# Recurrent attention beside a gated MLP: another order of loads and relays ahead of the first scores

## The chip, the cores and the metric

The kernel runs on one core of a Trainium2 chip. The time is device microseconds of that core; lower is better. Three runs of the kernel before took 367.76, 369.17 and 369.84 us, with a median of 369.17 us. One further execution was profiled. It took 366.92 us, and the span from its first to its last instruction is 364.8 us. The engines are named as in the profile: PE is TensorE's matmul and PEld its weight load, DVE is VectorE, ACT is ScalarE, POOL is GpSimd, SP is SyncE. SPq and ACTq are the queues of SP and ACT that issue DMAs.

## The reference

The input x has 2048 rows of 640 in bf16. Rows are normalized, and two branches read them. Branch A is attention with 32 heads of 20 in 4 segments of 512 rows: causal softmax within a segment, and a memory M, z that earlier segments left. Branch B is a gated MLP of width 1536.

```
xn = layernorm(x)
# branch A, for each segment s (512 rows):
logits = qs @ ks.T * scale + causal mask;  a_dot = softmax(logits) @ vs
a_mem  = (phi(qs) @ M) / (phi(qs) @ z + 1e-6)      # phi(t) = t + 1 if t > 0 else exp(t)
o      = g * a_mem + (1 - g) * a_dot               # g = sigmoid(beta), one number a head
M += phi(ks).T @ vs;  z += sum(phi(ks))
s = concat(o) @ wo
# branch B:
h = sigmoid(xn @ w_gate) * (xn @ w_up);  g = silu(h @ w_down)
out = x + s * g
```

## The kernel before, in words

The program is one straight list of instructions for each engine; an engine works through its list in order. The source emits the instructions, and their order in the source is their order on each engine. Two parts emit them: `startup()` (L514 to L557) by hand, for what comes ahead of the first scores, and the loop at L607, which walks 4 segments x 24 slots. A slot emits one `scores` unit, then fill work, then `weigh` of the unit before. Fill work has two sources: a heap of tasks with a due time in slots (`at`, `later`) and the list `bulk` of `gate`, `up` and `down` pieces. `take(k)` emits the first k pieces of `bulk` at once.

The names that matter here:

- `x_load(n, p)` (L105) loads rows of segment n: two chunks of 128 rows x 640 (160 KB each) as two DMAs for segment 0, as one DMA of 320 KB for later segments. Segment 0's four chunks are issued on SP's queue. Wv (800 KB) and beta are issued on ACT's queue, Wk and Wq (800 KB each), the first third of w_gate (`Wg[0]`) and of w_up (`Wu[0]`) (640 KB each) on SP's (L115 to L131). All these stand at the very start of both queues.
- `warm()` runs WARM = 36 matmuls of the identity on PE, ahead of the first real ones.
- `ln_stats` is five small DVE and POOL steps for each chunk: two halves of statistics (L199, L200), their sum (L201), and the reciprocal root on POOL (L202, L203). `ln_norm` writes the normalized chunk xn (L210). In segment 0, PE transposes it (L217) and ACT copies it to xnT (L218); in later segments a DMA transpose on SP's queue does (L220).
- `v_pair` emits the v projection (L305), `k_chunk` (L244) and `q_chunk` (L269) those of K and Q; ACT copies the results in segment 0 (L233, L309).
- The scores need Q and K with another assignment of rows to partitions, and this goes through DRAM: `stage_out` stores K or Q in two parts (L258), `relay` loads each half back in four DMAs of 80 KB (L229) into KT or QT. Row 20 of each head's strip of QT holds a bound for the softmax: `q_bound` computes it on PE (L281) and ACT copies it to cb (L284); `c_out` stores it (L292, 32 KB) and `c_in` loads it into both QT tiles (L299). All of these DMAs are on SP's queue. The first scores (L459) read KT, QT and that row.
- `load_glu(i, which)` (L128) loads third i of w_gate or w_up. Pieces `gate(n, f)` and `up(n, f)` use third f // 4. `load_late` loads Wd (1920 KB) and Wo (800 KB).
- `gate` ends in a tanh on ACT (L380), `up` in a product on DVE (L390). `phi` is three steps on DVE and ACT for each of five chunks of K (L315, L316, L319, L323); its transposed result goes to `pkt` by DMA (L327).

In `startup()` SP's queue has this order after the first weights: both stores of K, relay of K half 0, `load_glu(1, 0)`, relay of K half 1, both stores of Q, relay of Q half 0, `c_out`, relay of Q half 1, `c_in`, `load_glu(1, 1)`, the rows of segment 1. PE has, behind the last q chunk: `v_pair(3)`, `q_bound`, then three gates and three ups of `bulk` (`take(1)`, `take(5)`), then the first scores.

Each DMA counts its landing on one of eight semaphores. The framework deals them out in turn, over both queues, and a DMA that is given one waits until the DMA that had it before has landed.

Of the kernel before, what the change touches and what calls it, by code (L numbers as in the profile page):

```python
# [9 lines left out]
P = 128  # L10
# [3 lines left out]
DH = 20  # L14
# [29 lines left out]
    [(2, 0, 256, 256)],  # L44
]

WARM = 36
SHARE = (1.15, 1.15, 0.7)
NSLOT = NG * len(UNITS)

# [2 lines left out]
def kernel(  # L53
# [14 lines left out]
    nc = tc.nc  # L68
    x2 = A_x.flatten_outer_dims()
# [16 lines left out]
    Cs = [dpool.tile([H, L], BF, name=f"Cs{i}") for i in range(2)]  # L86
# [8 lines left out]
    def at(time, cost, fn, *a):  # L95
        count[0] += 1
        heapq.heappush(tasks, (time, count[0], cost, fn, a))

    def later(lag, fn, *a):
        at(clock[0] + lag, 0.0, fn, *a)  # L100
# [4 lines left out]
    def x_load(n, p):  # L105
        t = lnp.tile([P, 2, D], BF, name="xt2")
        st[n][f"x{p}"] = t
        r0 = n * L + 2 * p * P
        if n == 0:
            for i in range(2):  # L110
                nc.sync.dma_start(t[:, i, :], x2[r0 + i * P:r0 + (i + 1) * P, :])
        else:
            nc.sync.dma_start(t[:], x2[r0:r0 + 2 * P, :].rearrange("(i p) d -> p i d", p=P))

    x_load(0, 0)  # L115
    x_load(0, 1)
    W = {}
    beta_b = cpool.tile([P, H], BF, name="beta_b")
# [7 lines left out]
    def load_glu(i, which):  # L126
        w, src = ((Wg, B_w_gate), (Wu, B_w_up))[which]
        nc.sync.dma_start(w[i][:], src[:, i * L:(i + 1) * L].rearrange("(c p) n -> p c n", p=P))  # L128
# [20 lines left out]
    QT = [cpool.tile([P, 4, L], BF, name=f"QT{i}") for i in range(3)]  # L149
# [5 lines left out]
    def v_ones(a, b):  # L155
        for i in range(a, b):
            nc.gpsimd.memset(V[i][:, :, DH:VW], 1.0)

    def make_ind():

        nc.gpsimd.memset(nInd[:], -1.0)
        nc.gpsimd.affine_select(out=nInd[:], in_=nInd[:], compare_op=ALU.is_ge, fill=0.0,
                                base=0, pattern=[[P, DC], [-DH, H]], channel_multiplier=1)
        nc.gpsimd.affine_select(out=nInd[:], in_=nInd[:], compare_op=ALU.is_ge, fill=0.0,
                                base=DH - 1, pattern=[[-P, DC], [DH, H]], channel_multiplier=-1)
# [24 lines left out]
    def ln_stats(n, p, i0=0, i1=2):  # L190
        s = st[n]
        x = s[f"x{p}"]
        if i0 == 0:
            s[f"mv{p}"] = lnp.tile([P, 2, 2], F32, name="mv")
            s[f"rstd{p}"] = lnp.tile([P, 2], F32, name="rstd")
        mv, rstd = s[f"mv{p}"], s[f"rstd{p}"]
        for i in range(i0, i1):
            bs = lnp.tile([P, 2, 6], F32, name="bs")
            nc.vector.bn_stats(bs[:, 0, :], x[:, i, 0:HB])  # L199
            nc.vector.bn_stats(bs[:, 1, :], x[:, i, HB:D])  # L200
            nc.vector.bn_aggr(mv[:, i, :], bs[:])  # L201
        nc.gpsimd.tensor_scalar(rstd[:, i0:i1], mv[:, i0:i1, 1], EPS, None, op0=ALU.add)  # L202
        nc.gpsimd.tensor_tensor(rstd[:, i0:i1], rstd[:, i0:i1], nhalf[:, i0:i1], op=ALU.pow)  # L203

    def ln_norm(n, p, i):
        s = st[n]
        if "xnT" not in s:
            s["xnT"] = xpool.tile([P, DC, L], BF, name="xnT")
        xn = lnp.tile([P, D], BF, name="xn")
        nc.vector.tensor_scalar(xn[:], s[f"x{p}"][:, i, :], s[f"mv{p}"][:, i, 0:1], s[f"rstd{p}"][:, i:i + 1],  # L210
                                op0=ALU.subtract, op1=ALU.mult)
        j = 2 * p + i
        dst = s["xnT"][:, :, j * P:(j + 1) * P]
        if n == 0:
            pT = ps_d.tile([P, DC, P], BF, name="pT", tag="d")
            for c in range(DC):
                nc.tensor.transpose(pT[:, c, :], xn[:, c * P:(c + 1) * P], ident[:])  # L217
            nc.scalar.copy(dst, pT[:])  # L218
        else:
            later(0.7, lambda: nc.sync.dma_start_transpose(dst, xn[:]))  # L220


    def half_tile(tiles, n, half):
        return tiles[(2 * n + half) % 3]

    def relay(n, half, src, dst):
        rows = src[n % 2].rearrange("(g r d) n -> r d g n", r=4, d=DH)
        for r in range(4):
            nc.sync.dma_start(half_tile(dst, n, half)[32 * r:32 * r + DH, :, :], rows[r][:, 4 * half:4 * half + 4, :])  # L229
# [26 lines left out]
    def stage_out(n, half, src, dst, name):  # L256
        a, b = ((0, 3), (3, 5))[half]
        nc.sync.dma_start(src[n % 2][a * P:b * P, :].rearrange("(c p) n -> p c n", p=P), st[n][name][:, a:b, :])  # L258
        if n:
            later(1.0, relay, n, half, src, dst)  # L260
# [28 lines left out]
            c_out(n, cb)  # L289

    def c_out(n, cb):
        nc.sync.dma_start(Cs[n % 2][:, :], cb[:])  # L292
        if n:
            later(1.0, c_in, n)

    def c_in(n):
        rows = Cs[n % 2].rearrange("(g r) n -> r g n", r=4)
        for half in range(2):
            nc.sync.dma_start(half_tile(QT, n, half)[DH:P:32, :, :], rows[:, 4 * half:4 * half + 4, :])  # L299

    def v_tile(n, j, half):
        s = st[n]
# [197 lines left out]
    def take(k):  # L500
        for _, fn, a in bulk[:k]:
            fn(*a)
        del bulk[:k]

    def warm():
        ps = ps_d.tile([P, L], F32, name="wps", tag="d")
        for i in range(WARM):
            nc.tensor.matmul(ps[:, 0:P], lhsT=ident[:], rhs=ident[:], start=True, stop=True)

    def v_pair(j):  # L510
        for h in range(2):
            v_tile(0, j, h)

    def startup():  # L514
        warm()
        nc.gpsimd.memset(KT[0][:], 1.0)
        ln_stats(0, 0, 0, 1)
        ln_stats(0, 0, 1, 2)
        ln_norm(0, 0, 0)
        v_ones(0, 4)  # L520
        ln_stats(0, 1, 0, 1)
        ln_norm(0, 0, 1)
        v_pair(0)
        ln_stats(0, 1, 1, 2)
        ln_norm(0, 1, 0)
        v_pair(1)
        ln_norm(0, 1, 1)
        v_pair(2)
        make_ind()
        nc.gpsimd.memset(KT[1][:], 1.0)  # L530
        for c in range(DC):
            k_chunk(0, c)
        nc.gpsimd.memset(KT[2][:], 1.0)
        stage_out(0, 0, Ks, KT, "k5")
        for c in range(DC):
            q_chunk(0, c)
            if c == 0:
                stage_out(0, 1, Ks, KT, "k5")
                relay(0, 0, Ks, KT)
                load_glu(1, 0)  # L540
            elif c == 2:
                relay(0, 1, Ks, KT)
                stage_out(0, 0, Qs, QT, "q5")
        make_bd()
        v_ones(4, 8)
        v_pair(3)
        stage_out(0, 1, Qs, QT, "q5")
        relay(0, 0, Qs, QT)
        q_bound(0)
        relay(0, 1, Qs, QT)  # L550
        c_in(0)
        take(1)
        gates()
        take(5)
        load_glu(1, 1)
        x_load(1, 0)
        x_load(1, 1)  # L557

    startup()
    at(0.9, 0, load_glu, 2, 0)  # L560
# [5 lines left out]
    for n in range(NSEG):  # L566
        w = NSLOT * n
        m = n + 1
        if m < NSEG:
            for p in range(2):  # L570
                at(w + 0.2 + 3 * p, 0.1, ln_stats, m, p)
                for i in range(2):
                    at(w + 1.2 + 3 * p + 0.3 * i, 0.1, ln_norm, m, p, i)
            for i in range(8):
                at(w + (5.2 if i < 4 else 6.2) + 0.5 * i, 0.68, v_tile, m, i // 2, i % 2)
            for c in range(DC):
                at(w + 9.6 + 0.75 * c, 1.08, k_chunk, m, c)
                at(w + 13.4 + 0.75 * c, 1.08, q_chunk, m, c)
                at(w + 12.6 + 0.8 * c, 0.0, phi, m, "k5", c)
                at(w + 18.8 + 0.7 * c, 0.0, phi, m, "q5", c)  # L580
            at(w + 17.2, 1.12, q_bound, m)
            if m + 1 < NSEG:
                for p in range(2):
                    at(w + 16.1 + p, 0.0, x_load, m + 1, p)
            if n == 0:
                for c in range(DC):
                    at(0.3 + 0.8 * c, 0.0, phi, 0, "k5", c)
            for i, cs in enumerate(([0, 1, 2], [3, 4])):
                at(w + 8.9 + i, 0.6, m_update, n, cs)
        if n >= 1:  # L590
            for j in range(4):
                at(w + 1.1 + 0.3 * j, 0.0, o_ready, n - 1, j)
                if j < 2:
                    at(w + 4.0 + j, 0.0, xr_load, n - 1, j)
            for i in range(8):
                at(w + 6.6 + i, 0.68, o_proj, n - 1, i // 2, i % 2)
                at(w + 3.0 + 0.75 * i, 0.35, mem_read, n, i // 2, i % 2)
# [52 lines left out]
    n = NSEG - 1  # L650
# [43 lines left out]
```

## Time and profile before

| what | us |
|---|---|
| median of three runs | 369.17 |
| the profiled execution | 366.92 |
| its span | 364.8 |
| PE busy in the span | 340.2 |
| ACT busy | 234.6 |
| DVE busy | 228.2 |
| POOL busy | 103.7 |
| first statistics on DVE (row chunk 0 there) | 3.24 |
| first v matmul on PE | 10.29 |
| first K matmul on PE | 16.73 |
| first Q matmul on PE | 22.13 |
| first scores on PE | 40.06 |
| second, third scores on PE | 43.93, 49.33 |

A row of the timeline has its start, its duration, the engine, the line in the kernel, the operation with output and input, how many of them were merged, and in brackets the time that the engine sat idle before it with what ended that. Line numbers are those of the kernel before. A span on PE is modelled at its end, so a busy PE is not PE at its peak. The page's slices are each a fortieth of the span, 9.12 us.

### The profile page before, as it was taken

Reading aid. Unit: us, or ns where it says so; the run is one execution under the profiler, and the core shown is the slowest. Engines: PE = TensorE matmul, PEld = TensorE weight load, DVE = VectorE, ACT = ScalarE, POOL = GpSimd, SP = SyncE. Lnnn points to the kernel's source line nnn. Section 1 sums busy time; section 2 is a strip of 40 time slices with the busy share of each in tenths; the row PEclk is TensorE's granted clock in tenths of the full one; section 3 lists DMA queues with packets and bytes.
Section 4 is the critical chain, followed back from the end, with each engine's and each line's share of the span. In section 5 each row is a group of like instructions: output and inputs, shape, how many; then the busy total and the mean of one; then the engine's idle time right before and its main releaser. Section 6 shows DMA issues by size and latency. Waiting matters only on the chain.

```text
span 364.8 us, 8458 instructions
## 1 busy us (share of the span) xinstructions
PE 340.2 (93%) x3404; PEld 190.2 (52%) x3404; DVE 228.2 (63%) x579; ACT 234.6 (64%) x267; POOL 103.7 (28%) x180
## 2 busy tenths in 40 slices
PE   5999679999999999999999999999999999999972
PEld 4644234554565456644466456644466455545751
DVE  3252186379656587899655887889664576433353
ACT  2554278667797666657687667547677877777530
POOL 5830034222323332213222432122222233322200
PEclk9999899999999999999999999999999999999998
DMA  6847769413830460144910361143620311200003
GB/s 223 265 122 203 233 159 312 83 43 107 207 86 3 92 90 20 56 129 103 201 49 2 71 91 22 57 125 95 158 48 0 64 48 56 66 25 2 2 2 107
DMA packets 53606, 34.89 MB, mean 96 GB/s; under 512 B 28992, under 2 KB 53568, under 8 KB 53568
## 3 DMA queue, kind: packets, MB, share of 16 engines
q1 hardware_dynamic: 52768, 33.53, 36.6%
q10 hardware_dynamic: 800, 0.83, 0.7%
q8 instruction: 26, 0.43, 0.5%
q14 instruction: 12, 0.10, 0.1%
HBM read 19.80 MB, written 8.00 MB: 76 GB/s over the span
## 4 chain that ended last, share of the span: by engine, by line
PE 66%; DVE 11%; DMA 9%; ACT 8%; issue 2%; POOL 2%; SPq 1%; ACTq 0%; DVEq 0%
PE yp L400 13%; PE up L387 9%; PE gp L377 9%; PE Aps L484 6%; ACT pt L465 6%; PE Sps L459 6%; PE psk L244 6%; PE psv L305 5%; PE psq L269 4%; PE sp L439 4%; DMA xt<-in_A_x_dram 3%; POOL pt L467 2%; DMA xnT<-xn 2%; DMA Qs<-q 2%; DVE hT L390 1%
## 5 line engine op out<-in xcount | busy, mean ns | idle before, releaser
L465 ACT ACTIVATE pt<-Sps 128x2048 bf16<-128x2048 f32 (+1 forms) x96 | 152.7, 1591 | 44.8 <-PE Sps L459 42.1
L467 POOL TENSOR_SCALAR_AFFINE_SELECT pt<-pt 128x512 bf16<-128x512 bf16 x128 | 82.0, 652 | 225.0 <-ACT pt L465 225.0
L387 PE MATMUL up<-xnT,Wu 128*128 128x512 bf16 x240 | 60.8, 384 | 0.4 <-DVE om L367 0.4
L377 PE MATMUL gp<-xnT,Wg 128*128 128x512 bf16 x240 | 60.1, 381 | 0.0
L400 PE MATMUL yp<-Wd,hT 128*128 128x320 bf16 x384 | 57.0, 299 | 0.0
L484 PEld LDWEIGHTS <-pt 128*128 128x128 bf16 x1280 | 43.8, 96 | 19.9 <-issue 4.1
L390 DVE SCALAR_TENSOR_TENSOR hT<-tg,up 128x512 bf16<-128x512 bf16 x48 | 32.7, 681 | 31.8 <-PE up L387 31.0
L484 PE MATMUL Aps<-va,pt 128*128 128x21 bf16 x1280 | 48.1, 173 | 2.0 <-DVE od L493 1.2
L400 PEld LDWEIGHTS <-hT 128*128 128x128 bf16 x384 | 35.3, 97 | 14.6 <-issue 2.0
L459 PE MATMUL Sps<-QT,KT 21*128 21x128 bf16 (+3 forms) x512 | 35.1, 304 | 8.3 <-ACT pt L465 4.9
L380 ACT ACTIVATE tg<-gp 128x512 bf16<-128x512 f32 x48 | 28.6, 595 | 15.6 <-PE gp L377 15.3
L404 DVE SCALAR_TENSOR_TENSOR aa<-t,yp 128x320 bf16<-128x320 bf16 x32 | 15.6, 486 | 35.8 <-ACT t L403 35.8
L387 PEld LDWEIGHTS <-Wu 128*128 128x128 bf16 x240 | 21.0, 98 | 22.7 <-issue 2.8
L377 PEld LDWEIGHTS <-Wg 128*128 128x128 bf16 x240 | 20.5, 97 | 23.4 <-issue 3.7
L459 PEld LDWEIGHTS <-KT 21*128 21x128 bf16 x512 | 11.5, 91 | 37.0 <-issue 35.2
L319 ACT ACTIVATE mn<-mn 128x512 bf16<-128x512 bf16 x35 | 22.0, 629 | 11.2 <-DVE mn L315 11.2
L305 PE MATMUL psv<-Wv,xnT 128*128 128x320 bf16 x160 | 28.0, 312 | 0.1
L439 PE MATMUL sp<-Wo,oT 128*128 128x320 bf16 x160 | 26.1, 298 | 0.4 <-ACT oT L421 0.4
L403 ACT ACTIVATE t<-yp 128x320 bf16<-128x320 f32 x32 | 13.9, 435 | 17.7 <-PE yp L400 17.7
L269 PE MATMUL psq<-xnT,Wq 128*128 128x512 bf16 x100 | 24.2, 379 | 0.5 <-DVE hT L390 0.5
L244 PE MATMUL psk<-xnT,Wk 128*128 128x512 bf16 x100 | 24.2, 379 | 0.0
L309 ACT CAST va<-psv 128x320 bf16<-128x320 f32 x32 | 13.7, 427 | 13.2 <-PE psv L305 13.0
(72 smaller groups left out, 327.3 us busy)
## 6 DMA issues: line engine op xcount, KB each, us to landing
KT<-Ks SPq DMA_DIRECT2D x32, 80.0 KB
QT<-Qs SPq DMA_DIRECT2D x32, 80.0 KB
xr<-in_A_x_dram SPq DMA_DIRECT2D x16, 160.0 KB
out_dram<-xr SPq DMA_DIRECT2D x16, 160.0 KB
Wg<-in_B_w_gate_dram SPq DMA_DIRECT2D x3, 640.0 KB
Wu<-in_B_w_up_dram SPq DMA_DIRECT2D x3, 640.0 KB
xt<-in_A_x_dram SPq DMA_DIRECT2D x6, 320.0 KB
Wd<-in_B_w_down_dram SPq DMA_DIRECT2D x1, 1920.0 KB
```

The costliest lines, as they stand in the source:

```text
L244: nc.tensor.matmul(ps[:], lhsT=W["k"][:, k, c * P:(c + 1) * P], rhs=s["xnT"][:, k, :], start=(k == 0), stop=(k == DC - 1))
L269: nc.tensor.matmul(ps[:], lhsT=W["q"][:, k, c * P:(c + 1) * P], rhs=s["xnT"][:, k, :], start=(k == 0), stop=(k == DC - 1))
L305: nc.tensor.matmul(ps[:], lhsT=s["xnT"][:, k, j * P:(j + 1) * P], rhs=W["v"][:, k, half * HB:(half + 1) * HB], start=(k == 0), stop=(k == ...
L377: nc.tensor.matmul(gp[:], lhsT=Wg[f // 4][:, k, fo:fo + P], rhs=s["xnT"][:, k, :], start=(k == 0), stop=(k == DC - 1))
L387: nc.tensor.matmul(ps[:], lhsT=Wu[f // 4][:, k, fo:fo + P], rhs=s["xnT"][:, k, :], start=(k == 0), stop=(k == DC - 1))
L390: nc.vector.scalar_tensor_tensor(out=h[:], in0=s["tg"][:], scalar=1.0, in1=ps[:], op0=ALU.add, op1=ALU.mult)
L400: nc.tensor.matmul(yp[:], lhsT=s["hT"][f][:, j * P:(j + 1) * P], rhs=W["d"][:, f, hs], start=(f == 0), stop=(f == FC - 1))
L439: nc.tensor.matmul(sp[:], lhsT=s[f"oT{j}"][:, c, :], rhs=W["o"][:, c, hs], start=(c == 0), stop=(c == DC - 1))
L459: nc.tensor.matmul(Sps[:, r, c0:c0 + ncol], lhsT=kt[32 * r:32 * r + VW, g % 4, kb * P:(kb + 1) * P], rhs=qt[32 * r:32 * r + VW, g % 4, q0: ...
L465: nc.scalar.activation(pt[:, :, 0:ntot], Sps[:, :, 0:ntot], ACT.Exp, scale=SCALE)
L467: nc.gpsimd.affine_select(out=pt[:, :, c0:c0 + P], in_=pt[:, :, c0:c0 + P], compare_op=ALU.is_ge, fill=0.0, base=0, pattern=[[0, 4], [1, P ...
L484: nc.tensor.matmul(A[:, qb, r, :], lhsT=pt[:, r, off:off + P], rhs=V[4 * (n % 2) + kb][:, 4 * g + r, :], start=first, stop=True, skip_grou ...
```

## The change

The four row chunks of segment 0 are issued on two queues, two on SP and two on ACT, and Wv and beta stand behind ACT's two. In segment 0, `c_out` and `c_in` move to ACT's queue, and `c_in` moves in the source behind `take(1)`, `gates()` and two more pieces. `load_glu(1, 0)` leaves its place between the relays of K; it, the rows of segment 1 and `load_glu(1, 1)` now follow the relays of Q. Five pieces of `bulk` are taken ahead of the first scores and not six, and there are four more warm-up matmuls. The tasks `ln_stats` and `ln_norm` for segment 1 are due 1.5 slots later; those of later segments stay.

```diff
@@ -44,7 +44,7 @@
     [(2, 0, 256, 256)],
 ]
 
-WARM = 36
+WARM = 40
 SHARE = (1.15, 1.15, 0.7)
 NSLOT = NG * len(UNITS)
 
@@ -108,7 +108,7 @@
         r0 = n * L + 2 * p * P
         if n == 0:
             for i in range(2):
-                nc.sync.dma_start(t[:, i, :], x2[r0 + i * P:r0 + (i + 1) * P, :])
+                (nc.sync, nc.scalar)[p].dma_start(t[:, i, :], x2[r0 + i * P:r0 + (i + 1) * P, :])
         else:
             nc.sync.dma_start(t[:], x2[r0:r0 + 2 * P, :].rearrange("(i p) d -> p i d", p=P))
 
@@ -289,14 +289,15 @@
             c_out(n, cb)
 
     def c_out(n, cb):
-        nc.sync.dma_start(Cs[n % 2][:, :], cb[:])
+        (nc.sync if n else nc.scalar).dma_start(Cs[n % 2][:, :], cb[:])
         if n:
             later(1.0, c_in, n)
 
     def c_in(n):
         rows = Cs[n % 2].rearrange("(g r) n -> r g n", r=4)
         for half in range(2):
-            nc.sync.dma_start(half_tile(QT, n, half)[DH:P:32, :, :], rows[:, 4 * half:4 * half + 4, :])
+            (nc.sync if n else nc.scalar).dma_start(half_tile(QT, n, half)[DH:P:32, :, :],
+                                                    rows[:, 4 * half:4 * half + 4, :])
 
     def v_tile(n, j, half):
         s = st[n]
@@ -537,7 +538,6 @@
             if c == 0:
                 stage_out(0, 1, Ks, KT, "k5")
                 relay(0, 0, Ks, KT)
-                load_glu(1, 0)
             elif c == 2:
                 relay(0, 1, Ks, KT)
                 stage_out(0, 0, Qs, QT, "q5")
@@ -548,13 +548,15 @@
         relay(0, 0, Qs, QT)
         q_bound(0)
         relay(0, 1, Qs, QT)
-        c_in(0)
+        load_glu(1, 0)
+        x_load(1, 0)
+        x_load(1, 1)
+        load_glu(1, 1)
         take(1)
         gates()
-        take(5)
-        load_glu(1, 1)
-        x_load(1, 0)
-        x_load(1, 1)
+        take(2)
+        c_in(0)
+        take(2)
 
     startup()
     at(0.9, 0, load_glu, 2, 0)
@@ -567,10 +569,11 @@
         w = NSLOT * n
         m = n + 1
         if m < NSEG:
+            lag = 0.0 if n else 1.5
             for p in range(2):
-                at(w + 0.2 + 3 * p, 0.1, ln_stats, m, p)
+                at(w + lag + 0.2 + 3 * p, 0.1, ln_stats, m, p)
                 for i in range(2):
-                    at(w + 1.2 + 3 * p + 0.3 * i, 0.1, ln_norm, m, p, i)
+                    at(w + lag + 1.2 + 3 * p + 0.3 * i, 0.1, ln_norm, m, p, i)
             for i in range(8):
                 at(w + (5.2 if i < 4 else 6.2) + 0.5 * i, 0.68, v_tile, m, i // 2, i % 2)
             for c in range(DC):
```

## The prediction

> **What bounds the kernel now.** I read the page's busy table and its slices first. TensorE (PE) is busy for 340.2 of 364.8 us, and no other engine comes near.
>
> ```profile
> span 364.8 us, 8458 instructions
> PE 340.2 (93%) x3404; PEld 190.2 (52%) x3404; DVE 228.2 (63%) x579; ACT 234.6 (64%) x267; POOL 103.7 (28%) x180
> PE   5999679999999999999999999999999999999972
> DMA  6847769413830460144910361143620311200003
> ```
>
> The reader is to see that PE has two low places: the first slice, and the slices from 36 to 50 us. A table by stages gives their sizes (columns: stretch, its length, busy us and instructions of each engine, clock, DMA share, GB/s).
>
> ```profile
> 36.00:40.00 4.00, 0.81 (x4) 0.28 (x3) 0.69 (x1) 0.42 (x1) 0.00 (x0) 1.00 0.38 119
> 47.30:49.40 2.10, 0.08 (x5) 0.10 (x4) 2.02 (x6) 2.10 (x3) 0.56 (x2) 1.00 0.47 144
> 50.00:80.00 30.00, 29.11 (x317) 15.83 (x315) 17.78 (x45) 22.23 (x27) 10.10 (x16) 1.00 0.59 138
> ```
>
> From 50 us on PE is 97% busy, so what is won or lost before 50 us reaches the end undiminished. The chain of waits in order of time says what holds PE until then (start, length, what):
>
> ```profile
> 1.70 6.55 DMA xt<-in_A_x_dram
> 10.49 2.67 PE psv L305 x10
> 13.69 1.57 PE psv L305 x10
> 15.54 1.36 PE psv L305 x10
> 27.13 6.30 DMA Qs<-q
> 34.99 2.64 DMA Cs<-cb
> 39.44 5.11 DMA xt<-in_A_x_dram
> ```
>
> Four waits: for the rows; for the store of Q; for the bound's way through DRAM; for the next segment's rows. Ten equal v matmuls take 2.67, then 1.57, then 1.36 us: PE runs at half speed until about 14 us, although the page writes its clock as 9 there. The timeline shows PE's two stops and who ends them (idle before, releaser, in brackets):
>
> ```profile
> 40.06 0.40 PE L459 MATMUL Sps<-QT,KT 21*128 21x512 bf16 x4 [3.25 <-DMA QT<-Cs]
> 44.57 0.49 DVE L199 BATCH_NORM_STATS2 bs<-xt 128x6 f32<-128x320 bf16 x1 [6.96 <-DMA xt<-in_A_x_dram]
> 46.89 0.63 ACT L319 ACTIVATE mn<-mn 128x512 bf16<-128x512 bf16 x1 [3.96 <-DVE mn L315]
> 49.33 0.29 PE L459 MATMUL Sps<-QT,KT 21*128 21x256 bf16 x4 [2.02 <-ACT pt L465]
> 58.71 0.85 PE L305 MATMUL psv<-Wv,xnT 128*128 128x320 bf16 x5
> ```
>
> The second stop comes through three engines: DVE waits for rows, ScalarE (ACT) for DVE, PE for ACT.
>
> **The start.** The trace's landing events put the four row chunks at 3.22, 6.03, 8.25 and 8.71 us, and the v weights, issued at 0.78, at 5.68: the second chunk, issued at 1.23, came after all of them, and the third and fourth after beta (7.82). Transfers are served about in order of issue. Behind them Wk and Wq land 2.27 us apart (10.98, 13.25), so 160 KB cost 0.45 us. With rows first, the chunks land at 3.2, 3.7, 4.1 and 4.6. Wk and Wv then follow, one at 6.9, the other at 9.1. Which is first can't be read; the nearest row is the first pair, where SP's chunk (issued 0.79) went ahead of ACT's Wv (0.78), so I take Wk first. The v matmuls start at Wv's 9.1 plus 0.2 instead of 10.29: gain 1.0 (2.3 if Wv goes first, since the second transpose then ends at 8.0; 0.7 if Wv takes the 2.46 that it took after 3.22).
> [...]
> DVE is no new bound: statistics 1.05 (8.28 to 9.33) and norm 0.4 per chunk, from 3.24, put the last norm at 9.3 (rstd on POOL takes 0.9 of that) instead of 11.85. The two row issues put 0.85 us ahead of ACT's table load (1.85 to 3.13), which then ends at 4.0; ACT's first copy is due at 6.6. Uncovered they would cost 0.85. The four added warm-up matmuls (36 took 4.02 us, so 0.45) end at 5.9, when the first normalized chunk is ready; uncovered, 0.45.
> Clock: if all thirty v matmuls and the two transposes among them ran at the last rates, 1.31 + 0.21 + 0.25 = 1.8 us would go; PE is now busier ahead of them (1.44 to 6.6 almost without a gap), so I take half, 0.9; the other bound is a loss of 1.3 (the second group at 2.67 too, and some of a transpose).
> [...]
> Start in all: -1.9. All that follows moves by it; the times below are on the old clock, before that shift.
>
> **The relays.** Now SP carries Qs, four relays, the bound, four relays, the bound back. Taking Wg1 (640 KB) out ahead of Qs should land Qs near 30 (Ks took 2.52) instead of 33.43. But the built order shows what the diff doesn't: eight landing semaphores are dealt out in turn, and in the changed program SP's first relay of Q waits for the lane of the bound's store, the fourth (L229) for the lane of the bound's load on ACT's queue. So the relay can't run ahead of the bound. The bound's store goes at cb's end, 30.9, and lands 2.64 later at 33.5. Its load stands on ACT behind the second gate's tanh (33.61 + 0.60), goes at 34.25, lands 2.32 later (37.70 to 40.02) at 36.57. Then SP issues relay four, which lands 2.26 later (33.45 to 35.70): first scores at 38.9, not 40.06. PE has by then one unit less behind it (take 5, not 6: 1.08 us), so this part alone gives nothing: 1.16 - 1.08. The load's issue takes 1.2 us of ACT; behind it stands the third tanh, due at 35.5 anyway.
> Behind that wait on SP stand three relays, Wg1, both rows, Wu1, Wg2, Wu2. Wg1 goes at 38.4; by the old spacing (first load 4.70 after issue, rows 0.92 each, a weight 1.88) they land at 43.1, 44.0, 44.9, 46.8, 48.7, 50.6.
> The lag of 1.5 slots puts the statistics behind the fourth hT on DVE, so the stop at 47.3 goes. What is late next is Wu1: PE's order is scores, up, gate, scores, up, A, gate (Wg1, ends 44.8, or 46.5 at half clock), then the fifth up, at 46.8. It takes 1.2; third scores at 48.0 against 49.33, with the same PE work done: -1.3. Bounds: with no wait for Wu1 -3.1; with relay four as slow as KT's while Wg1 was in flight (5.91, not 2.26), 3.65 later, +2.3.
>
> **Behind the third scores.** The next segment's first transpose now stands on SP behind Wd (1920 KB), where it stood ahead. Wd starts after Wu2 and one transpose, 51.2, and takes 5.6 at the rate of the weights or 7.35 as it did (53.98 to 61.33); then pkt's and this one, 0.6 each: 58.0 to 59.7. PE wants it 9.4 us after the third scores (49.33 to 58.71), less 0.3: 57.1. Cost 0.9 to 2.6; 0.4 if PE arrives later; I take 1.4. The third transpose, awaited 0.31 at 67.06, comes when Wo is through: -0.3. The rest of PE's work is the same, in nearly the same order.
>
> **Sum.** -1.0 - 0.9 - 1.3 + 1.4 - 0.3 = -2.1. The profiled execution took 366.92 (span 364.8); 364.8 by the sum. The median of the runs is 369.17, 2.25 above the profiled one, so the time to compare is 369.17 - 2.1 = 367.1.
>
> **Rivals.**
> 1. Wv is served before Wk: v starts at 8.0, 1.3 more. For: both are issued within a few hundredths of a us. Against: SP won the first pair. 365.8.
> 2. The gain is given back: no clock gain, the transpose 2.6 late: -1.0 - 1.3 + 2.6 - 0.3 = 0. 369.2. For: DMA is at 1.0 of its share from 41 to 48 already. Against: the whole stop at 47.3 goes.
> 3. Slower: relay four hangs on the bound, and its landing is the place. At KT's 5.91 first scores come at 42.6; the loads behind it on SP move too, so the 3.65 come in full: -2.1 + 3.65 = +1.55, 370.7, and with the bound's load 0.8 slower too, as another row of relays took (3.12 against 2.32), 371.5. It decides once first scores come more than 2.1 later than 38.9. Against: Wg1 is no longer in flight there.
>
> **How the numbers follow.** Forecast 0.40, rival one 0.18, two 0.24, three 0.18. The time is the forecast's, 367.1. Its own range takes the bounds of clock (0.9 either way) and transpose (-1.0, +1.2): 365.2 to 369.2. The full range reaches down to rival one with the whole clock gain and half of the transpose's (365.8 - 0.9 - 0.5) and up to rival three: 364.4 to 371.5. A measurement of this kernel can tell about 0.5%, 1.85 us, from no change. Of the forecast 0.25 of 0.40 lies below 367.3, of rival one all, of rival two 0.06: faster 0.49; of rival three 0.14, with 0.05 from the rest: slower 0.19; the same 0.32.
>
> **What would show it.** Right: DVE's four statistics without a wait for rows after the first; v matmuls from about 9.3; first scores near 37 and third near 46, with a DMA wait for Wu1 ahead of the fifth up; a DMA wait for xnT ahead of the next segment's first v. Wrong: Q's relay issued before the bound has landed; v waiting beyond 10; a longer stop at the first scores; or PE idle after 50 us in new places.

## The result, and the profile after

The changed kernel takes 372.49 us (median of five executions, 371.84 to 374.00); the kernel before, 369.17. The ratio over all executions is 1.0107, with a 95% interval of 1.0082 to 1.0132 (the two medians alone give 1.0090): about 1% slower, where 367.1 us and a gain of 2.1 were predicted, with 371.5 as the upper end.

One caution for the reading. The profiled execution after, 374.00, is the longest of its five; the profiled one before, 366.92, was shorter than each of the timed ones. So the two traces lie 7.1 us apart, and the medians 3.3. In what follows the traces say where time goes, and the ratios of many executions say how much.

The page of the changed kernel, its span, the busy row of the engines and the slices of PE and of DMA:

```profile
span 371.8 us, 8423 instructions
PE 341.1 (92%) x3365; PEld 191.4 (51%) x3408; DVE 230.9 (62%) x579; ACT 235.4 (63%) x267; POOL 103.8 (28%) x180
PE   6799886999999999999999999999999999999982
DMA  8625699503670145132950152132630221110003
```

PE's low places have moved: before they were slices one, five and six, the rows and the two stops; now slices one and two are low, and the seventh (from 55.8 us). From the eighth on PE is as full as before. The chain of waits in order of time (start, length, what) names them:

```profile
1.71 9.72 DMA Wv<-in_A_wv_dram
11.56 2.83 PE psv L306 x10
14.92 2.61 PE psv L306 x10
34.67 2.25 DMA QT<-Qs
41.69 7.29 DMA Wu<-in_B_w_up_dram
54.40 7.30 DMA xnT<-xn
```

At the start it is no longer the rows that the chain waits for but Wv. Then come Q's relay, Wu1 and, new, the next segment's transpose. The timeline of PE (start, length, instruction, in brackets the idle time before it and who ended it):

```profile
11.56 2.83 PE L306 MATMUL psv<-Wv,xnT 128*128 128x320 bf16 x10 [3.47 <-DMA Wv<-in_A_wv_dram]
...
19.00 1.24 PE L244 MATMUL psk<-xnT,Wk 128*128 128x512 bf16 x4
...
38.16 0.39 PE L460 MATMUL Sps<-QT,KT 21*128 21x512 bf16 x3 [0.16 <-DMA QT<-Cs]
40.11 0.37 PE L460 MATMUL Sps<-QT,KT 21*128 21x512 bf16 x1 [1.55 <-DMA QT<-Qs]
...
49.02 1.25 PE L388 MATMUL up<-xnT,Wu 128*128 128x512 bf16 x5 [1.69 <-DMA Wu<-in_B_w_up_dram]
50.21 0.29 PE L460 MATMUL Sps<-QT,KT 21*128 21x256 bf16 x4
...
61.75 1.51 PE L306 MATMUL psv<-Wv,xnT 128*128 128x320 bf16 x5 [3.63 <-DMA xnT<-xn]
```

The reader is to see four DMA waits of 3.47, 1.55, 1.69 and 3.63 us, where the kernel before had two long stops. The table by stages (stretch, length, busy us and instructions of each engine, clock, DMA share, GB/s) adds what follows the first and the last of them:

```profile
10.50:17.30 6.80, 5.74 (x25) 3.46 (x26) 0.00 (x0) 1.98 (x4) 6.53 (x10) 0.50 0.74 249
36.00:41.00 5.00, 3.28 (x17) 1.12 (x15) 1.19 (x3) 1.55 (x3) 0.00 (x0) 1.00 0.35 103
48.90:50.80 1.90, 1.77 (x23) 0.88 (x24) 0.52 (x2) 0.19 (x1) 0.94 (x2) 1.00 1.09 349
61.70:65.10 3.40, 3.35 (x25) 1.76 (x26) 0.45 (x1) 0.43 (x1) 0.37 (x1) 0.50 0.87 194
88.95:116.55 27.60, 26.18 (x283) 15.28 (x283) 20.71 (x53) 22.03 (x26) 7.74 (x12) 1.00 0.52 124
```

In the first and the fourth row the granted clock is 0.50: each of these two waits is followed by a stretch in which PE does its work at half speed, which costs half of its busy time there, an estimated 2.9 and 1.7 us. (Not all of the 2.9 is new: the kernel before had its first ten v matmuls at half speed too, 2.67 us where its third ten took 1.36, against 2.83 here.) The last row is 27.60 us for what took 26.47 before; more on it below.

Where the 7.1 us between the two traces lie is read at points that have the same number of gates and ups behind them in both programs:

| point on PE or ACT | before | after | difference | since the point above | the prediction's terms |
|---|---|---|---|---|---|
| first K matmul | 16.73 | 19.00 | +2.27 | +2.27 | -1.0 - 0.9 |
| third scores | 49.33 | 50.21 | +0.88 | -1.39 | -1.3 |
| 14th exp | 83.11 | 88.95 | +5.84 | +4.96 | +1.4 - 0.3 |
| 23rd exp | 109.58 | 116.55 | +6.97 | +1.13 | none |
| last exp | 340.70 | 347.67 | +6.97 | 0 | none |

### The profile page after: what moved, and what is told of

Same layout as the page of the kernel before. It is cut to its first block, busy times and chain, and to the rows that moved or that the text cites. A ratio compares the mean times of both kernels' runs of the same rounds, so it can differ in the third digit from the quotient of the medians.

```text
span 371.8 us, 8423 instructions
## 1 busy us (share of the span) xinstructions
PE 341.1 (92%) x3365; PEld 191.4 (51%) x3408; DVE 230.9 (62%) x579; ACT 235.4 (63%) x267; POOL 103.8 (28%) x180
## 4 chain that ended last, share of the span: by engine, by line
PE 64%; DVE 11%; DMA 10%; ACT 9%; issue 2%; POOL 2%; SPq 1%; ACTq 0%; DVEq 0%
PE yp L401 13%; PE up L388 9%; PE gp L378 8%; ACT pt L466 8%; PE psv L306 7%; PE Aps L485 6%; PE Sps L460 6%; PE psk L244 5%; PE sp L440 4%; PE psq L269 3%; DMA Wv<-in_A_wv_dram 3%; POOL pt L468 2%; DMA xnT<-xn 2%; DMA Wu<-in_B_w_up_dram 2%; DVE q L235 2%
## 5 line engine op out<-in xcount | busy, mean ns | idle before, releaser
L388 PE MATMUL up<-xnT,Wu 128*128 128x512 bf16 x229 | 59.6, 385 | 2.7 <-DMA Wu<-in_B_w_up_dram 1.7
L306 PE MATMUL psv<-Wv,xnT 128*128 128x320 bf16 x160 | 29.6, 326 | 7.1 <-DMA xnT<-xn 3.6
```

Source lines behind the costliest of these rows:

```text
L306: nc.tensor.matmul(ps[:], lhsT=s["xnT"][:, k, j * P:(j + 1) * P], rhs=W["v"][:, k, half * HB:(half + 1) * HB], start=(k == 0), stop=(k == ...
L388: nc.tensor.matmul(ps[:], lhsT=Wu[f // 4][:, k, fo:fo + P], rhs=s["xnT"][:, k, :], start=(k == 0), stop=(k == DC - 1))
```

## The experiments

All ratios are to the kernel before, run beside each of them on the same chip; its median there was 369.23 (29 executions), 368.87 (31) and 368.82 (29). "Theory A" in the first expectations is the reading of the trace above: the start is lost through Wv, and behind the third scores the transposes wait for Wd.

**Splitting the change.** First the start alone: the kernel before with the diff's lines on WARM and on the rows.

```diff
-WARM = 36
+WARM = 40
-                nc.sync.dma_start(t[:, i, :], x2[...])
+                (nc.sync, nc.scalar)[p].dma_start(t[:, i, :], x2[...])
```

> The kernel before with the first part of the change alone: rows 2 and 3 on ACT's queue ahead of Wv, 40 warm-up matmuls. Theory A (the start is a loss: Wk and Wv now run beside each other and land together): first v at 11.5, first K at 18 to 19 where before had 16.73, time 370.5 to 371.5. Rival (the start is a gain, as predicted, and all the loss lies behind the relays): first v at 9.3, time 367.3.

Then the rest alone: the changed kernel with these two lines undone.

> The changed kernel with its start as before (all four row chunks on SP, 36 warm-up matmuls); relays, bound on ACT, later loads and later statistics stay. Theory A: first K at 16.7; third scores about 1.4 earlier than before for the same PE work; then 3 to 4.6 lost at the next segment's first v, which waits for a transpose behind Wd: 370 to 371.5. Rival (the relays' wait for the bound is the loss): third scores later than before, no long wait at that v; 372.5.

Measured: the start alone 370.39 us, ratio 1.0031 (1.0007 to 1.0056); the rest alone 371.73 us, 1.0057 (1.0040 to 1.0074). Both halves lose, 1.15 and 2.1 us, and in sum (0.88%) they make the change's loss within its interval. In the prediction the start was to gain 1.9 and the rest 0.2. The start's trace has the changed kernel's wait:

```profile
10.86 2.56 PE L305 MATMUL psv<-Wv,xnT 128*128 128x320 bf16 x9 [2.35 <-DMA Wv<-in_A_wv_dram]
```

The trace of the rest alone is not what Theory A expected. It has no wait for a transpose at that v, and its third scores come at 50.65, later than before (49.33). Ahead of them PE waits for Wg1 and Wu1, and five matmuls that take 1.24 us at 39.64 take 2.32 and 2.31, half speed:

```profile
44.69 2.32 PE L378 MATMUL gp<-xnT,Wg 128*128 128x512 bf16 x5 [1.89 <-DMA Wg<-in_B_w_gate_dram]
48.41 2.31 PE L388 MATMUL up<-xnT,Wu 128*128 128x512 bf16 x5 [1.40 <-DMA Wu<-in_B_w_up_dram]
50.65 0.40 PE L460 MATMUL Sps<-QT,KT 21*128 21x256 bf16 x4
```

That is what the rival expected to see. The cause that it names, the relays' wait for the bound, is tried below: with Wv first, taking that wait away gained nothing.

**The start: which queue carries Wv.** The prediction held that transfers are served in order of issue. That has a basis in the trace before: from 3.0 to 4.5 us its DMA rows (queue, packets, MB, share of the engines; q1 is SP's queue, q10 ACT's) have Wv alone, though SP had issued its second chunk at 1.23:

```profile
q10 hardware_dynamic: 427, 0.55, 100.9%
```

The changed kernel from 5 to 10 us, with Wk and Wv under way:

```profile
q1 hardware_dynamic: 718, 0.90, 53.5%
q10 hardware_dynamic: 652, 0.78, 46.6%
```

Here the engines serve both side by side, and nearly 1600 KB must pass before either is whole: by the trace's landing events Wk came at 10.33 and Wv at 11.43. If that is the loss, Wv ahead of Wk on one queue must land early. In the changed kernel (beta moves too; the two rows above add up to 100.1% of the engines, so they did not stand still for its small packets):

```diff
-    for name, src, eng in (("v", A_wv, nc.scalar), ("k", A_wk, nc.sync), ...):
+    for name, src, eng in (("v", A_wv, nc.sync), ("k", A_wk, nc.sync), ...):
-    nc.scalar.dma_start(beta_b[:], A_beta.partition_broadcast(P))
+    nc.sync.dma_start(beta_b[:], A_beta.partition_broadcast(P))
```

> The changed kernel with Wv issued on SP ahead of Wk, and beta behind Wq, so that nothing runs beside Wv. Theory A: Wv lands near 7.2, first v at 8.0 to 8.2, first K at 13 to 14.5 where the changed kernel had 19.0; 4 less than the changed kernel, 368.5. Rival (transfers are served in order of issue whatever the queue, and Wv was late for another reason): Wv later than 9, time 372.

Measured: 368.55 us, 0.9994 (0.9967 to 1.0021), 1.1% under the changed kernel. Wv landed at 8.10 and Wk at 10.35, and PE ran from there at full speed (granted clock 1.00 from 8.2 to 13.0):

```profile
8.23 1.52 PE L306 MATMUL psv<-Wv,xnT 128*128 128x320 bf16 x10
9.59 0.44 PE L217 MATMUL pT<-ident,xn 128*128 128x128 bf16 x5
9.87 1.52 PE L306 MATMUL psv<-Wv,xnT 128*128 128x320 bf16 x10
```

The same edit on the start alone:

> Kernel before, with the rows on both queues, 40 warm-up matmuls, and Wv on SP's queue ahead of Wk (beta behind Wq); nothing else of the change. Theory A (the start loses only because Wk and Wv, on two queues, share the DMA engines): Wv lands near 7.9 us, first v matmul near 8.2, first K scaling some 3.5 us earlier than before; Q's store moves with it, but the fourth relay of KT and Wg1's load keep their place behind one another, so of the 3.5 some 2 us reach the end: 367 (ratio 0.994). Rival (the clock, not the order of weights, sets the start: v runs earlier but at half speed for as much longer): 369 (1.000). Rival (the rows behind, the bound's load and Wg1, are due at fixed times, so the start's gain is waited away at the second stop): 369, with first scores earlier and third scores as before.

Measured: 366.88 us, 0.9955 (0.9926 to 0.9984). The gain is there, though not all of it: in its trace the bound's way through DRAM ends a longer wait ahead of the first scores (3.25 us before):

```profile
39.43 0.61 PE L459 MATMUL Sps<-QT,KT 21*128 21x512 bf16 x4 [4.66 <-DMA QT<-Cs]
```

Is ACT's queue only served behind SP's? For that the startup was run alone (all behind the pieces ahead of the first scores left out), in three forms.

> The startup of the changed kernel alone (all that follows the pieces ahead of the first scores is left out, and rows of Wv are written as the output): Wk on SP's queue, Wv on ACT's, as in the change. It should show the changed kernel's start: Wk and Wv land within some 1.1 us of each other, Wv last, at 10 to 11.5; first v matmul after 10.3. Its time is not to be compared with the whole kernel's.

> The same startup alone with Wv on SP's queue and Wk on ACT's. Sharing (the two queues are served side by side, packet by packet): Wv still lands at 9.8 or later and within about 1.2 of Wk, the first v matmul waits for it to 10 or later. Rival (SP's queue is served ahead of ACT's): Wv lands near 8, Wk some 2.3 behind, v starts at 8.2.

> The same startup alone with both on SP's queue, Wv first and beta behind Wq: Wv lands between 7.8 and 9.6, as in the five whole kernels with this start, and Wk 2.2 to 2.3 behind it (both theories; it is the case to compare with).

| startup alone | Wv lands | Wk lands | first v matmul | PE waited for Wv |
|---|---|---|---|---|
| Wv on ACT, Wk on SP (the change) | 12.23 | 11.09 | 12.37 | 4.10 |
| Wv on SP, Wk on ACT | 10.37 | 13.88 | 10.50 | 2.29 |
| both on SP, Wv first | 9.57 | 12.00 | 9.71 | 1.40 |

Each row is one execution. Sharing holds: on SP's queue, with Wk beside it, Wv is at 10.37 and not near 8. From 5 to 10 us the two queues had 669 and 568 packets there, so SP's had somewhat more, and Wk came 3.5 behind Wv, not within 1.2 as expected: Wq, next on SP's queue, had taken Wv's place beside it. The landings of one order differ between executions: Wv in front of Wk on one queue landed between 7.82 and 9.64 in nine traces, so tenths are not to be read from one of them; the three rows here differ by 0.8 and 1.9. Over all traces the two cases do not overlap: with Wk beside it on the other queue, Wv landed between 10.37 and 12.23 in five.

**Behind the third scores: Wd.** The trace's largest wait was put to the test by calling Wd's load later, in the changed kernel.

```diff
-    at(2.6, 0, load_late, "d", B_w_down)
+    at(3.8, 0, load_late, "d", B_w_down)
```

> The changed kernel with Wd due 1.2 slots later, which puts it on SP's queue behind the next segment's first two transposes. Theory A: no wait for a transpose at that v (3.6 gone, and the half clock behind it, 1.0): 368. Rival (PE would have waited there for something else, or Wd only moves its wait to the third transpose): 371 to 372.5.

Measured: 373.42 us (six executions), 1.0113 (1.0082 to 1.0144): no gain. In its trace the wait of 3.63 is gone, and the third transpose, now behind Wd, is waited for:

```profile
69.87 0.85 PE L306 MATMUL psv<-Wv,xnT 128*128 128x320 bf16 x5 [1.29 <-DMA xnT<-xn]
```

So this wait has another size in each trace (3.63 in the changed kernel, none with the rest alone, 1.19 with Wv first), and by these runs the ratio doesn't rest on it. What the wait is worth by itself isn't shown, since a part of it came back at the third transpose.

**The piece that was taken out.** With the rest alone and in every trace with five pieces ahead of the first scores, the stretch from the 14th to the 23rd exp takes 27.6 us instead of 26.5, at the same work of PE. The sixth piece was put back, in the kernel with Wv first:

```diff
         c_in(0)
-        take(2)
+        take(3)
```

> Kernel after with Wv ahead of Wk on SP (the run before of that name gave ratio 0.999), and six pieces again ahead of the first scores instead of five (the last take of 2 becomes 3). Theory B (the piece that was taken out is paid twice: PE idles at the first scores instead of doing it, and it is done later): PE's idle time at the first scores falls by about 1.1 us, first scores stay within 0.3, and every exp behind them comes about 1.1 earlier: ratio 0.996 to 0.997. Rival C (PE's wait there is only moved: the sixth piece needs Wg1 or comes after the relays' landing, so first scores come 1.1 later): ratio 0.999 to 1.000.

Measured: 367.05 us, 0.9950 (0.9917 to 0.9983), against 0.9994 without the piece. And in the rest alone:

> Kernel after with the start undone (that run gave ratio 1.0057), and six pieces again ahead of the first scores instead of five. Theory D (the rest of the change loses by the piece that it takes out of the wait for the first scores, 1.1 us, and by the changed order behind it, 1.1 us of idle time of PE between the 14th and the 23rd exp; the relays and the next segment's transposes come out even, as predicted): these slots take 26.5 us as in the kernel before, not 27.6, and the ratio is 0.999 to 1.001. Rival E (the loads behind Q's relays make the loss: Wg1, Wu1 and Wd late): the sixth piece only lengthens the way to the first scores or the wait for Wg1, ratio 1.004 to 1.006.

Measured: 368.78 us, 1.0002 (0.9977 to 1.0028), against 1.0057. Within these intervals the piece is the whole loss of the rest: 0.55%, 2.0 us, nearly twice its own time of 1.08. The stretch in question by stages, five pieces:

```profile
86.18:113.79 27.61, 26.40 (x285) 15.29 (x283) 20.75 (x53) 22.05 (x26) 7.80 (x12) 1.00 0.51 123
```

Six pieces:

```profile
84.91:111.41 26.50, 26.21 (x283) 15.18 (x283) 18.76 (x52) 21.88 (x26) 7.61 (x12) 1.00 0.55 135
```

PE is busy 26.40 and 26.21 us (two records are missing from the second), and idle 1.21 and 0.29. What it waits for with five pieces, in the timeline of the rest alone:

```profile
88.12 0.29 PE L460 MATMUL Sps<-QT,KT 21*128 21x256 bf16 x4 [0.47 <-ACT pt L466]
97.34 0.29 PE L460 MATMUL Sps<-QT,KT 21*128 21x256 bf16 x4 [0.48 <-ACT pt L466]
```

With six pieces neither wait is there. The loop deals the remaining pieces out to slots by a budget; one piece more in the list shifts which slot each falls into, and in two slots the scores come so soon that ACT's exp of the unit before is not done. The beginnings and ends of the two stretches give the account: with the same work behind it, the six-piece trace is 1.27 us ahead at the 14th exp (84.91 against 86.18) and 2.38 at the 23rd (111.41 against 113.79). The 1.1 us between them is the idle time, and it is in every trace: the stretch takes 27.6 us in all five with five pieces and 26.5 in all seven with six. How the first 1.27 comes about isn't shown. At the third scores, where both have ten pieces behind them, the six-piece trace is 0.52 ahead (50.13 against 50.65), although its waits for DMA there sum to 5.68 us against 5.16. Behind them the rest alone runs at half speed until 54.9 us and the six-piece trace until 52.3 (granted clock 0.50 from 44.6 and from 45.5), so the clock has a share in it.

**The relays and Wg1.** Four tries to shorten the waits for Q, Wg1 and Wu1, all with Wv first. The bound on POOL's queue, where it has landing semaphores of its own (three in that run's program, which no DMA of SP or ACT uses), so that Q's relays don't wait for it:

```diff
-        (nc.sync if n else nc.scalar).dma_start(Cs[n % 2][:, :], cb[:])
+        (nc.sync if n else nc.gpsimd).dma_start(Cs[n % 2][:, :], cb[:])
```

(the same in `c_in`).

> Kernel after with Wv ahead of Wk, and the first bound's store and loads issued on POOL's queue instead of ACT's, so that SP's relays of Q share no landing semaphore with the bound. Theory B (the rest of the change loses because SP's first and fourth relay of Q wait for the bound, and Wg1, the rows and Wu1 stand behind them): SP's first relay goes within 0.3 us of Qs's landing, the first three strips' scores come some 2 us earlier, Wg1 is issued 2 to 4 us earlier, and PE's waits for Wg1, Wu1 (1.15 and 2.37 in the run without it) fall below 1 in sum: ratio 0.993 to 0.995. Rival C (the loads are bound by what the DMA engines move, so that issuing earlier only slows the relays beside them): first scores within 1 us, ratio 0.998 to 1.001.

Measured: 368.73 us, 1.0002 (0.9971 to 1.0034): nothing. Q's relay went right behind Qs's landing, at 26.68, and Wg1 at 29.72, but the bound's first load, issued at 30.36 behind Wg1, landed at 36.81, with the first scores behind it:

```profile
36.85 0.61 PE L460 MATMUL Sps<-QT,KT 21*128 21x512 bf16 x4 [5.27 <-DMA QT<-Cs]
```

In the changed kernel SP waited 1.8 us for the bound's store and 2.3 for its first load, and Wg1 went at 40.17, 4.2 behind the issue of that load (35.94); here, with no semaphore shared, it goes ahead of the load. With the sixth piece and the later Wd too:

> Kernel after with Wv ahead of Wk, the bound on POOL's queue, six pieces ahead of the first scores, and Wd later (slot 3.8 instead of 2.6). If the three losses add up (pieces 1.1, relays 2 to 3, the next segment's transpose 1 to 2): ratio 0.987 to 0.990, 364.5 to 365.5. If they are one loss that only moves from wait to wait: 0.996 to 0.999.

Measured: 371.46 us, 1.0068 (1.0035 to 1.0101), a miss on both sides: the trace has waits of 4.1 us for a transpose behind the later Wd and of 1.7 for Wv, which landed at 9.64 in it. The gains don't add. That the later Wd makes the loss is read from this one trace; no run takes it out. Last, Wg1 ahead of Q's first relay, with six and with eight pieces:

```diff
         stage_out(0, 1, Qs, QT, "q5")
+        load_glu(1, 0)
         relay(0, 0, Qs, QT)
         q_bound(0)
         relay(0, 1, Qs, QT)
-        load_glu(1, 0)
```

> Six pieces and Wv first (ratio 0.995; waits there: QT 1.3, Wg1 1.8, Wu1 1.6), with Wg1's load issued on SP just ahead of Q's first relay instead of behind the fourth relay's wait for the bound. Theory (Wg1, the rows, Wu1 are late only because they stand behind that wait): Wg1 lands before 35, the waits for Wg1 and Wu1 fall below 1 in sum, Q's relays land up to 2 later, ratio 0.991 to 0.994. Rival (what the weight gains, the relays lose, as both move through the same DMA engines): first scores 2 to 3 later, ratio 0.995 to 0.998.

> The same with eight pieces ahead of the first scores. If PE waits 2 to 3 us for Q there, the two pieces take its place: ratio 0.988 to 0.991. Rival (the next up stands still for Wu1, or the order behind turns ragged): as with six pieces or worse, 0.995 and more.

Measured: 367.90 us, 0.9977 (0.9944 to 1.0010), and 370.01 us, 1.0036 (1.0007 to 1.0066). With six pieces Wg1 landed at 35.27, not before 35, Q's last relay at 41.90 instead of 38.24, Wu1 at 46.31 instead of 44.05: what the weight won, the relays lost. With eight pieces PE reaches the fifth up sooner and waits 5.5 us for Wu1.

**A version that beats both.** The start with Wv first alone keeps Wg1 between K's relays, where it lands at 30.2 to 30.6, and has a wait of 4.66 us for the bound. Two more pieces go into it:

```diff
-        take(5)
+        take(7)
```

> The start with Wv first alone (ratio 0.9955; PE waited 4.7 us for the bound's relay), with eight pieces ahead of the first scores instead of six, all that the first loads of Wg and Wu allow. Theory D (a piece put into that wait is worth its own time, 1.08): the wait falls to some 2.5, first scores stay, ratio 0.989 to 0.991. Rival (the fifth up then comes at once and waits for Wu1, which landed at 42.8, or the order behind turns ragged as with five pieces): ratio 0.994 to 0.997.

Measured: 365.15 us (six executions, 362.38 to 366.42), 0.9895 (0.9847 to 0.9942). The wait fell by 2.37, twice a piece's time being 2.16, and a short one for Wu1 came:

```profile
39.89 0.40 PE L459 MATMUL Sps<-QT,KT 21*128 21x512 bf16 x4 [2.29 <-DMA QT<-Cs]
43.16 1.03 PE L387 MATMUL up<-xnT,Wu 128*128 128x512 bf16 x2 [0.71 <-DMA Wu<-in_B_w_up_dram]
```

## Why the prediction was wrong, by its own steps

**The start, -1.0 and -0.9: wrong in sign, and the step that failed.** The rows landed about as said, at 3.42, 3.63, 4.57 and 4.75. "Transfers are served about in order of issue" was read from one weight against one 160 KB chunk, which did stand still behind it; "Wk and Wv then follow, one at 6.9, the other at 9.1" carried this over to two weights. These shared the engines, and landed at 10.33 and 11.43. The v matmuls started at 11.56, not 9.3. The clock term fell with it: the granted clock was 1.00 early, from 7.1 us, but 0.50 from 10.5 to 17.3, in and behind the wait of 3.47 us. No run shows the 0.9 of that term: that a PE kept busier ahead of the v matmuls has them sooner at full speed was the author's estimate. With 40 warm-up matmuls and Wv in front on one queue, the first ten took 1.52 us in one trace and 2.67 in another; in the changed kernel two groups of ten took 2.83 and 2.61, against 2.67 and 1.57 before, which is near the loss of 1.3 that the text had as its other bound. Alone this part costs 0.31%, 1.15 us. That Wv's place decides was in the text as rival one, but as a question of which comes first, not of both coming late; with Wv in front on one queue the whole start gained 0.45%, 1.7 us. That this is near the 1.9 forecast is chance: the forecast had Wk in front, and rival one priced Wv in front at 1.3 more, 3.2.

**The relays, -1.3: right in mechanism, in size only in this trace.** In the traces of both kernels landings are counted on eight semaphores, 23 or 24 DMAs on each. SP's first relay of Q went at 34.67, 0.02 after the landing of the bound's store, the fourth at 38.04, 0.02 after that of its first load. Moved by the start's +2.27, the forecast's first scores (38.9), Wu1 (46.8) and third scores (48.0) stand at 41.2, 49.1 and 50.3; measured were 40.11 for the last strip, 48.98 and 50.21. Rival three, which hung on a slow fourth relay, did not come: it landed at 40.07, 2.0 after its issue. But other traces don't bear the size out. From the first K matmul to the third scores the kernel before took 32.60 us and the changed kernel 31.21; the rest alone took 33.65, and with its sixth piece back 32.97, so +1.05 and +0.37 in place of -1.3. In these two Wg1 took 6.34 and 5.81 us from issue to landing, against the 4.70 of the sum and 5.15 in the changed kernel, and the fifth up ran at half speed (2.31 us in both, 1.25 in the changed kernel).

**Behind the third scores, +1.4 and -0.3: the mechanism was there, the size was not settled by it.** The transpose landed at 61.70, in the forecast's 58.0 to 59.7 moved by 2.27. PE came for it at 58.1, 7.9 and not 9.1 us behind the third scores, since with five pieces one up less stands ahead of it. The trace has 4.96 us there, from a wait of 3.63 and 3.4 us at half speed. But with this wait gone, and 1.29 us of it back at the third transpose, the ratio stayed at 1.0113, and the rest alone, with six pieces, gave 1.0002: over many executions it is not seen to be what the change costs.

**What the sum lacked: the place of the sixth piece.** It was priced once, 1.08 against the 1.16 that the first scores gained, and called nothing. It was followed only up to the third scores, where both programs have done the same. Behind them the changed one is a piece behind again in most slots until the 14th exp, and the order in the slots is another. Measured: 0.55%, 2.0 us; half of it is idle time between the 14th and the 23rd exp, which the prediction held for a stretch of the same work in nearly the same order; where the other half falls is not shown.

In sum: forecast -1.9 for the start and -0.2 for the rest; measured alone +1.15 and +2.1. With six pieces the rest gives +0.1 (1.0002, with 0.9 either way), so its other terms came out about even in the median, though not one by one in the traces. The 0.19 given to slower rested on the relay that hangs; the kernel got slower for two other reasons.

Left open: whether the change with nothing but its sixth piece restored loses as much as the sum says (it wasn't run in this form, only with the start undone and with Wv first), and which share of its median the transpose's wait has, since only one execution of each kernel has a trace.

## What to carry to other kernels

Two large transfers issued at one time on two queues shared the engines in every trace here, and the one wanted first landed at 10.37 to 12.23 us instead of 7.82 to 9.64: put it ahead of the other on the same queue, and don't carry an order read from a large and a small transfer over to two large ones. When work is taken out of a wait, follow the list that it goes back to until both programs have done the same work for good, since a scheduler that deals by budget can move every later piece. And put pieces into a wait only as far as their operands have landed: two more were worth 0.6% where Wg1 was early, and cost as much where the next weight was late (in both pairs the intervals just overlap).

## What the runs showed of the hardware that was not expected

Two queues with weights of 800 KB under way were served nearly packet for packet (718 and 652 in 5 us, and 642 of these 1370 came behind one of the other queue; in another run 669 and 568), while before a chunk of 160 KB on SP's queue got nothing for 1.5 us beside Wv on ACT's. What decides between the two the runs don't show.

In the kernel before, the engines all but stood still from 5.5 to 6.5 us, with three chunks of rows issued and not landed (the first of them landed at 6.03). The DMA rows of that stretch:

```profile
q1 hardware_dynamic: 24, 0.03, 8.4%
q10 hardware_dynamic: 71, 0.00, 3.9%
```

ACT's queue has 71 packets, 67 of them of 64 bytes, in it; beta, spread to 128 partitions, is the transfer that was under way there (issued at 1.27, landed at 7.82). That it holds up the rows on the other queue was not tried by itself.

Half speed of PE came behind the first scores' wait of 1.55 too (granted clock 0.50 from 41.3 to 44.6), and not behind Wu1's of 1.69. It differs between executions: the mean granted clock went from 0.972 to 0.985 over the five of the changed kernel.
